# Two PSUM accumulators of a fused attention and mixture kernel: from two banks of one tile to two tiles

## The chip, the core and the metric

The kernel runs on one NeuronCore of a Trainium2 chip. The metric is the device time of one execution in microseconds (us). Runs of this kernel agree closely: three of them lie between 1134.3 and 1134.82 us.

## What is computed

```python
# q, k, v: (4 batches, 8 heads, 576 tokens, 64), float32
scores = (q @ k.T) / 8
mask = scores >= (32nd largest score of the row)
attn = softmax(where(mask, scores, -1e9))
x = attn @ v                                  # 2304 tokens x 512 features
h = maximum(x @ w_in, 0)                      # 512 -> 2048
x = (h * h) @ w_out                           # 2048 -> 512
h = x @ w_in2                                 # 512 -> 2048
out = (h * clip(h + 3, 0, 6) / 6) @ w_out2    # 2048 -> 512, float32
```

## The kernel before, in words

**Number format.** Everything that TensorE (PE) multiplies is held as a high and a low fp16 half, so each product is three matmuls: high times high, high times low, low times high. The four weight matrices arrive as 64-bit numbers. VectorE (DVE) and GpSimd (POOL) turn them into fp32 (lines 372, 375, 431). PE then multiplies each slab with itself so that the matrix's scale can be found (`gram`, line 447). After that, PE and ScalarE (ACT) split the scaled slab into its halves (`w_split`: matmuls at lines 555 and 561, ACT at 558 and 564).

**Attention.** For a tile of 128 queries, PE makes the scores (lines 707 to 716). DVE finds the 32 largest of each row by MAX8 and MATCH_REPLACE8 (lines 754 to 762). ACT and POOL make mask, exponent and halves (lines 766 to 793), a transposing DMA on SP's queue turns them, and PE multiplies with v (line 811).

**The mixture layers.** The 2304 tokens are taken in 18 units of 128 rows; two of the units are put together from two tiles of 64 rows, so the reads of the first layer's accumulator count 20. For one unit and one layer, 4 groups of 4 slices run through these steps. PE makes `hb` (line 1046, 12 matmuls of 128x128 a slice). ACT, and in the second layer DVE, apply the nonlinearity (1053, 1055, 1058, 1061). ACT and POOL split it into `ghl` (1068, 1071). PE adds the slice into an accumulator of 512 fp32 columns (line 1078, three matmuls of 128x512 a slice, called one step below). The first layer's accumulator (m = 0, here accumulator 0) is read by ACT at line 959 (squares for the row scale), by ACT at line 283 (high half) and by DVE at line 287 (low half). A transposing DMA (line 967) then brings the two halves into `hl`, the second layer's operand. The second layer's accumulator (m = 1, accumulator 1) is read by ACT at line 1150, and its result is stored to the output.

**Where the accumulators live.** `acc_t` is one PSUM tile of two banks; `acc_t[:, 0, :]` is accumulator 0 and `acc_t[:, 1, :]` accumulator 1. While the weights are being prepared, the same two banks have other uses: `gram` collects in bank 1, and every third slab of the first two matrices is scaled in bank 0 (`bank = "acc0"` at line 551), read there by ACT.

**What sets the order.** A planner (`Plan.run`) decides once, from costs, priorities and the dependencies that it is given, in which order each engine's instructions are written. Its pools `acc0` and `acc1` are two separate resources. The tile framework underneath then puts the semaphore waits on the written instructions, from what each one reads and writes. Every engine works through its own list in order. On PE, first-layer steps of one unit and second-layer steps of another alternate, with the `hb` matmuls of both between them.

Of the kernel before, what the change touches and what calls it, by code (L numbers as in the profile page):

```python
# [9 lines left out]
F32 = mybir.dt.float32  # L10
F16 = mybir.dt.float16
BF16 = mybir.dt.bfloat16
I32 = mybir.dt.int32
U16 = mybir.dt.uint16
AF = mybir.ActivationFunctionType
# [4 lines left out]
P = 128  # L20
# [115 lines left out]
def tile_topk_attention_moe_moe2(  # L136
# [11 lines left out]
    nc = tc.nc  # L148
# [4 lines left out]
    NT, DM = out.shape  # L153
# [15 lines left out]
    ps = ctx.enter_context(tc.tile_pool(name="ps", bufs=1, space=PSUM))  # L169
# [47 lines left out]
    for name, n in (("av", 1), ("h", 2)):  # L217
        pool(name, n, [P, 512], F32, ps)

    acc_t = ps.tile([P, 2, 512], F32, name="acc")  # L220
    plan.pool(acc0=1, acc1=1)
    pool("S", SBUFS, [P, 2 * S], F32)
    pool("W", 2, [P, S], F32)
# [161 lines left out]
    def w_convert(i, n_, pn, par):  # L385

        loads = wload[i, n_]
        hm = kb(i, 2 * w_order(i)[n_], 2 * w_order(i)[n_] + 2)
        src = kb(PLACE[i][n_][0], 4 * PLACE[i][n_][1], 4 * PLACE[i][n_][1] + 4) if PLACE[i][n_] and is64 else []
        key = n_  # L390
        low = is64 and n_ % 4 < NPOOL[i] and (i < 3 or n_ < 9)
        last = loads
        if is64:
            steps = []

            def conv():
                parts = stage[i, n_]
                w_ = 512 // len(parts)
                if not steps:
                    mid = take("h", "cv")  # L400
                    for h_, words in enumerate(parts):
                        steps.append(bits_to_f32(home(i, n_)[:, w_ * h_:w_ * h_ + w_],
                                                 words.rearrange("p (n a) -> p n a", a=2), low,
                                                 mid[:, w_ * h_:w_ * h_ + w_]))
                for e_ in steps:
                    next(e_)

            c_ = c0_ = None
            for cost in (0.65, 0.66) if low else (0.65, 0.66, 0.66):
                c_ = task("DVE", cost, (f"conv{i}", key), conv, deps=[*loads, c_], reads=src, writes=hm,  # L410
                          alloc=[] if c_ else ["h"])
                c0_ = c0_ or c_
            last = [c_]
            free("h", c0_, c_)
            wconv.append(c_)
            keep_warm(c_, 16 * i + n_)
            if PLACE[i][n_] is None:
                for h_ in range(2):
                    free("stg", loads[h_], c_)
            if low:  # L420

                box = {}

                def low_bits():
                    box["t"] = take("stg").bitcast(I32)[:, 0:512]
                    top = stage[i, n_][0].bitcast(U16).rearrange("p (n a) -> p n a", a=4)[:, :, 1]
                    nc.scalar.activation(box["t"], top, AF.Copy, scale=2.0 ** -13)

                def add():
                    d = home(i, n_).bitcast(I32)  # L430
                    nc.gpsimd.tensor_tensor(d, d, box["t"], op=ALU.add)  # L431

                b_ = task("ACT", 0.52, (f"bits{i}", key), low_bits, deps=[c0_], reads=src, alloc=["stg"])
                a_ = task("POOL", 1.22, (f"add{i}", key), add, deps=[b_], writes=hm)
                free("stg", b_, a_)
                last = [a_]
        ngrp = 4 if i % 2 == 0 else 1
        per = 16 // ngrp
        j = n_ % per

        def gram():
            pn["t"] = acc_t[:, 1, :].rearrange("p (c n) -> p c n", c=4)

            top = home(i, n_).bitcast(BF16).rearrange("p (n a) -> p n a", a=2)[:, :, 1]
            for c in range(4):
                blk_ = top[:, c * P:(c + 1) * P]
                nc.tensor.matmul(pn["t"][:, c, :], blk_, blk_, start=(j, c) == (0, 0), stop=j == per - 1,
                                 skip_group_check=True)

        pn["g"] = task("PE", 0.4, (f"gram{i}", key), gram, deps=last + [pn.get("g", lastgram.get(i - 1))], reads=hm,  # L450
                       alloc=["acc1"] if j == 0 else [])
        lastgram[i] = pn["g"]
        if j == 0:
            pn["o"] = pn["g"]
# [68 lines left out]
    def w_split(i):  # L523


        def diagonal():
            nc.gpsimd.tensor_scalar(diag, ident, wsc[i][:, 0:1], 1.0, op0=ALU.mult, op1=ALU.mult)

        d_ = task("POOL", 0.3, ("norm", 0), diagonal, deps=[wchain[i]], writes=["diag"])
        for n_, s in enumerate(w_order(i)):  # L530
            hm = kb(i, 2 * s, 2 * s + 2)
            key = n_
            box = {}
            if SPE[i][n_ % 4] == "a":
                def scaled(x=home(i, n_), box=box):
                    box["t"] = take("stg")[:, 0:512]
                    nc.scalar.activation(box["t"], x, AF.Copy, scale=wsc[i][:, 0:1])

                def high(hi=wt[i][:, s, 0, :], box=box):
                    nc.scalar.activation(hi, box["t"], AF.Copy)  # L540

                def low(hi=wt[i][:, s, 0, :], lo=wt[i][:, s, 1, :], box=box):
                    nc.gpsimd.tensor_tensor(lo, box["t"], hi, op=ALU.subtract)

                t1 = task("ACT", 0.61, (f"high{i}", key), scaled, deps=[wchain[i]], reads=hm, alloc=["stg"])
                t2 = task("ACT", 0.52, (f"high{i}", key), high, deps=[t1], writes=hm)
                wsplit[i, s] = task("POOL", 1.11, (f"low{i}", key), low, deps=[t2], writes=hm[1:])
                free("stg", t1, wsplit[i, s])
                continue

            bank = "acc0" if i < 2 and n_ % 3 == 2 else "h"

            def scaled(x=home(i, n_), box=box, bank=bank):
                box["t"] = acc_t[:, 0, :] if bank == "acc0" else take("h", "wx")
                nc.tensor.matmul(box["t"], diag, x, start=True, stop=True)

            def high(hi=wt[i][:, s, 0, :], box=box):
                nc.scalar.activation(hi, box["t"], AF.Copy)  # L558

            def rest(hi=wt[i][:, s, 0, :], box=box):  # L560
                nc.tensor.matmul(box["t"], minus, hi, start=False, stop=True, skip_group_check=True)

            def low(lo=wt[i][:, s, 1, :], box=box):
                nc.scalar.activation(lo, box["t"], AF.Copy)  # L564

            t1 = task("PE", 0.95, (f"scaled{i}", key), scaled, deps=[d_], reads=[*hm, "diag"], alloc=[bank])
            t2 = task("ACT", 0.48, (f"high{i}", key), high, deps=[t1], writes=hm)
            t3 = task("PE", 0.22, (f"rest{i}", key), rest, deps=[t2], reads=hm[:1])
            t4 = task("ACT", 0.48, (f"high{i}", key), low, deps=[t3], writes=hm[1:])
            free(bank, t1, t4)  # L570
            wsplit[i, s] = t4
# [360 lines left out]
    def x2_operand(u):  # L932

        us, n = units[u], usize[u]
        several = len(us) > 1
        box = {}
# [15 lines left out]
        def rows(i):  # L952
            return slice(off[i], off[i] + nof[i])

        def square(i):
            if i == us[0]:
                box["ss"], box["yh"] = take("ss"), take("xh")
            r = rows(i)
            nc.scalar.activation(box["yh"][r, 0].bitcast(BF16), acc_t[r, 0, :], AF.Square, accum_out=box["ss"][r],
                                 **({"scale": T["px", i][r]} if several else {}))  # L960

        def total():
# [34 lines left out]
        free("h", t3, t4)  # L997
        lows = []
        for i in us:
            lows += split(DM, lambda r=rows(i): acc_t[r, 0, :], [lambda r=rows(i): box["yh"][r, 0]],  # L1000
                          [lambda r=rows(i): box["yh"][r, 1]], lambda i=i: (T["px", i] if several else box["s"])[rows(i)],
                          "d", (("yhigh", pos[1, u, 0]), ("ylow", pos[1, u, 0])), [t4])
        t6 = task("SP", 1.25, ("yflip", pos[1, u, 0]), flip, deps=lows, lat=WLAT)
# [23 lines left out]
    def group(m, u, g):  # L1027
# [45 lines left out]
        def acc(fi, chunks):  # L1073
            f = g * GF + fi
            gl = [box["g"][:, d, fi * n:(fi + 1) * n] for d in range(2)]
            o_ = acc_t[0:n, m, :]
            for a, d in PRODS:
                nc.tensor.matmul(o_, gl[d], wt[2 * m + 1][:, f, a, :], start=f == 0 and (a, d) == (0, 0),  # L1078
                                 stop=f == KF - 1 and (a, d) == PRODS[-1])
# [56 lines left out]
    def second_layer(u):  # L1136
# [10 lines left out]
        def evac(ch):  # L1147
            rows = min(P, n - ch * P)
            box["o", ch] = take("f", "o")
            nc.scalar.activation(box["o", ch][0:rows], acc_t[0:rows, 1 if n == P else ch, :], AF.Copy,  # L1150
                                 scale=box["oc"][0:rows])

        def store(ch):
# [225 lines left out]
```

## Time and profile before

| what | value |
|---|---|
| median of 3 runs | 1134.74 us (1134.3 to 1134.82) |
| the profiled execution's own time | 1135.86 us |
| its span, first to last instruction | 1134.0 us |
| PE busy | 1032.9 us, 91% |
| DVE, ACT, POOL busy | 83%, 76%, 71% |
| mean granted TensorE clock | 0.98 |

The profiled execution lies 1.12 us above the median of the runs. Busy time of PE is read with care: the ends of matmuls are modelled in the profile, and a record overlaps the start of the next one. An idle time "<-X" is the time in which the engine stood still until X released it.

### The profile page before, as it was taken

How to read it: one execution, taken by the hardware profiler on the slowest of the kernel's cores; microseconds unless marked ns; L12 is line 12 of the kernel's file. 1: busy time of each engine (PE TensorE's matmuls, PEld its weight loads, DVE VectorE, ACT ScalarE, POOL GpSimd, SP SyncE). 2: the span in 40 equal slices, each digit the busy share in tenths (PEclk: the TensorE clock that was granted, in tenths of full speed). 3: DMA queues.
4: the chain of work that ended last, by engine and by line, in shares of the span. 5: the costliest groups of instructions: out<-in, count | busy, mean ns of one | idle time of the engine just before them, and what ended most of it. 6: DMA issues, size and time to landing. Idle time of an engine off the chain costs nothing.

```text
span 1134.0 us, 31149 instructions
## 1 busy us (share of the span) xinstructions
PE 1032.9 (91%) x12407; PEld 723.9 (64%) x12407; DVE 939.9 (83%) x2026; ACT 866.8 (76%) x1600; POOL 802.0 (71%) x1041
## 2 busy tenths in 40 slices
PE   3436988889999999999999999999999999999998
PEld 1234446476766776677666767777767767777675
DVE  6999999999778999999989999986799989970010
ACT  6755989799898777888997878878967878773332
POOL 5798767589877677777887878777767867673221
PEclk9985999989999999999999999999999999999999
DMA  8978655224565424343754334434233332431100
GB/s 273 263 227 282 181 120 139 57 52 66 117 121 124 67 53 68 68 62 64 120 114 96 63 73 66 69 72 86 71 63 62 69 72 53 73 72 41 10 20 20
DMA packets 227905, 107.40 MB, mean 95 GB/s; under 512 B 210736, under 2 KB 210736, under 8 KB 227760
## 3 DMA queue, kind: packets, MB, share of 16 engines
q1 hardware_dynamic: 227760, 105.41, 43.0%
q8 instruction: 97, 1.59, 0.6%
q14 instruction: 48, 0.39, 0.1%
HBM read 48.76 MB, written 4.72 MB: 47 GB/s over the span
## 4 chain that ended last, share of the span: by engine, by line
PE 61%; ACT 15%; DVE 13%; issue 4%; POOL 3%; DMA 3%; SPq 0%; ACTq 0%; DVEq 0%; POOLq 0%
PE acc L1078 25%; PE hb L1046 25%; PE av L811 4%; DVE W L759 3%; PE sp L713 3%; DVE m L762 3%; ACT E L775 2%; ACT w L564 1%; DVE m L754 1%; ACT E L783 1%; ACT w L558 1%; DVE cv L372 1%; DVE w L375 1%; ACT wc L788 1%; POOL w L431 1%
## 5 line engine op out<-in xcount | busy, mean ns | idle before, releaser
L1046 PEld LDWEIGHTS <-w 128*128 128x128 f16 x6912 | 424.3, 98 | 105.3 <-issue 5.9
L1078 PE MATMUL acc<-w,ghl 128*128 128x512 f16 x1728 | 460.0, 379 | 12.0 <-DVE xh L287 5.6
L1046 PE MATMUL hb<-hl,w 128*128 128x128 f16 x6912 | 467.2, 220 | 4.0 <-ACT w L564 1.6
L762 DVE MAX8 m<-W 128x8 f32<-128x576 f32 x432 | 314.2, 749 | 1.8
L778 POOL TENSOR_TENSOR E<-S,E 128x576 f32<-128x576 f32 x144 | 203.3, 1414 | 50.6 <-ACT E L775 49.8
L1071 POOL TENSOR_TENSOR ghl<-r,ghl 128x512 f16<-128x512 f32 x144 | 167.3, 1162 | 100.4 <-ACT ghl L1068 88.4
L759 DVE MATCH_REPLACE8 W<-m,W 128x576 f32<-128x576 f32 x288 | 213.2, 742 | 0.0
L1078 PEld LDWEIGHTS <-ghl 128*128 128x128 f16 x1728 | 145.1, 98 | 100.1 <-issue 14.6
L792 POOL TENSOR_TENSOR wc<-E,wc 128x512 f16<-128x512 f32 x144 | 167.8, 1166 | 39.5 <-ACT wc L788 37.6
L775 ACT ACTIVATE E<-S,scalars 128x576 f32<-128x576 f32 x144 | 111.5, 775 | 35.6 <-POOL scalars L770 33.4
L783 ACT ACTIVATE E<-E,scalars 128x576 f32<-128x576 f32 x144 | 125.1, 869 | 17.0 <-POOL E L778 16.6
L754 DVE MAX8 m<-S 128x8 f32<-128x576 f32 x144 | 107.1, 748 | 22.6 <-ACT S L722 16.4
L1061 DVE SCALAR_TENSOR_TENSOR r<-r,hb 128x512 f32<-128x512 f32 x72 | 48.8, 678 | 78.2 <-ACT r L1055 77.3
L759 DVE MATCH_REPLACE8 W<-m,S 128x576 f32<-128x576 f32 x144 | 106.7, 742 | 0.0
L1068 ACT ACTIVATE ghl<-r 128x512 f16<-128x512 f32 x144 | 90.4, 628 | 19.9 <-DVE r L1061 17.0
L788 ACT ACTIVATE wc<-E 128x576 f16<-128x576 f32 x144 | 98.1, 681 | 0.7
L811 PEld LDWEIGHTS <-wT 128*128 128x128 f16 (+1 forms) x2240 | 82.4, 102 | 19.3 <-issue 6.5
L1055 ACT ACTIVATE r<-hb,bias,scalars 128x512 f32<-128x512 f32 x72 | 55.7, 774 | 47.3 <-PE hb L1046 43.6
L811 PE MATMUL av<-vv,wT 128*128 128x64 f16 (+1 forms) x2240 | 91.0, 196 | 0.7 <-DMA wT<-wc 0.7
L431 POOL TENSOR_TENSOR w<-w,stg 128x512 int32<-128x512 int32 x57 | 72.6, 1285 | 25.1 <-DVE w L375 9.2
L1053 ACT ACTIVATE r<-hb 128x512 f32<-128x512 f32 x72 | 43.1, 598 | 57.2 <-PE hb L1046 56.7
L726 ACT ACTIVATE S<-sp 128x1024 f32<-128x1024 f32 x64 | 65.3, 1020 | 14.5 <-POOL E L778 14.2
(113 smaller groups left out, 1208.2 us busy)
## 6 DMA issues: line engine op xcount, KB each, us to landing
w<-in_moe_w_in_dram SPq DMA_DIRECT2D x32, 512.0 KB, 6.4
w<-in_moe_w_out_dram SPq DMA_DIRECT2D x29, 512.0 KB, 4.2
stg<-in_k_dram SPq DMA_DIRECT2D x16, 320.0 KB, 3.2
stg<-in_v_dram SPq DMA_DIRECT2D x16, 320.0 KB, 3.8
stg<-in_q_dram SPq DMA_DIRECT2D x16, 288.0 KB, 3.9
out_dram<-o SPq DMA_DIRECT2D x16, 256.0 KB, 2.1
wT<-wc SPq DMA_TRANSPOSE x144, 3.3
stg<-in_moe_w_out_dram SPq DMA_DIRECT2D x6, 256.0 KB, 3.5
```

The source lines that it names most:

```text
L754: nc.vector.max(m[:, 0:8], scores())
L759: nc.vector.match_replace(out=T["W", s], in_to_replace=m[:, 8 * c - 8:8 * c], in_values=scores() if c == 1 else T["W", s], imm_value=-3.0e38)
L762: nc.vector.max(m[:, 4 * r:4 * r + 8], T["W", s])
L775: nc.scalar.activation(T["E", s], scores(), AF.Relu, bias=T["kb", s], scale=-FAR)
L778: nc.gpsimd.tensor_tensor(T["E", s], scores(), T["E", s], op=ALU.subtract)
L783: nc.scalar.activation(T["E", s], T["E", s], AF.Exp, bias=T["nb", s], scale=T["scl", b, hp], accum_out=T["sums", i][:, t:t + 1])
L788: nc.scalar.activation(T["wc", s][:, 0:S], T["E", s], AF.Copy)
L792: nc.gpsimd.tensor_tensor(wc[:, S + TAIL:], e[:, 0:S - TAIL], wc[:, 0:S - TAIL], op=ALU.subtract)
L811: nc.tensor.matmul(out_[cols, t * D:(t + 1) * D], wT[0:kr, a, cols], vv[0:kr, vb, hh, c, :], start=n_ == 0, stop=n_ == len(prods) - 1)
L1046: nc.tensor.matmul(box["h"][:, fi * n:(fi + 1) * n], wt[2 * m][:, kk * 4 + f // 4, a, f % 4 * P:(f % 4 + 1) * P], hl[:, c, kk, 0:n], start ...
L1071: nc.gpsimd.tensor_tensor(flat(box["g"][:, 1]), flat(box["r"]), flat(box["g"][:, 0]), op=ALU.subtract)
L1078: nc.tensor.matmul(o_, gl[d], wt[2 * m + 1][:, f, a, :], start=f == 0 and (a, d) == (0, 0), stop=f == KF - 1 and (a, d) == PRODS[-1])
```

## The change

`acc_t` becomes a list of two tiles of one bank each, and every use takes the tile that the index named before. The two tiles lie in the same two banks as before, and the planner is given the same tasks, so each engine's instructions come in the same order as before.

```diff
-    acc_t = ps.tile([P, 2, 512], F32, name="acc")
+    acc_t = [ps.tile([P, 512], F32, name=f"acc{m}") for m in range(2)]
...
-            pn["t"] = acc_t[:, 1, :].rearrange("p (c n) -> p c n", c=4)
+            pn["t"] = acc_t[1].rearrange("p (c n) -> p c n", c=4)
...
-                box["t"] = acc_t[:, 0, :] if bank == "acc0" else take("h", "wx")
+                box["t"] = acc_t[0] if bank == "acc0" else take("h", "wx")
...
-            nc.scalar.activation(box["yh"][r, 0].bitcast(BF16), acc_t[r, 0, :], AF.Square, accum_out=box["ss"][r],
+            nc.scalar.activation(box["yh"][r, 0].bitcast(BF16), acc_t[0][r], AF.Square, accum_out=box["ss"][r],
...
-            lows += split(DM, lambda r=rows(i): acc_t[r, 0, :], [lambda r=rows(i): box["yh"][r, 0]],
+            lows += split(DM, lambda r=rows(i): acc_t[0][r], [lambda r=rows(i): box["yh"][r, 0]],
...
-            o_ = acc_t[0:n, m, :]
+            o_ = acc_t[m][0:n]
...
-            nc.scalar.activation(box["o", ch][0:rows], acc_t[0:rows, 1 if n == P else ch, :], AF.Copy,
+            nc.scalar.activation(box["o", ch][0:rows], acc_t[1 if n == P else ch][0:rows], AF.Copy,
```

What differs in the built program is which instructions wait. In the lists below a name in brackets is the engine whose semaphore the instruction waits for (a name with DMA is a queue's). In the changed kernel `acc_99` is accumulator 0 and `acc_100` accumulator 1; `w_95` is the second layer's output matrix.

PE, in the middle of the mixture, a second-layer step; before:

```order
L1046 MATMUL hb<-hl,w_92 128x128
L1078 LDWEIGHTS ghl
L1078 MATMUL acc<-w_95,ghl 128x512 [waits Activation_49]
L1078 LDWEIGHTS ghl
L1078 MATMUL acc<-w_95,ghl 128x512
L1078 LDWEIGHTS ghl
L1078 MATMUL acc<-w_95,ghl 128x512
```

And in the changed kernel:

```order
L1046 MATMUL hb<-hl,w_92 128x128
L1078 LDWEIGHTS ghl
L1078 MATMUL acc_100<-w_95,ghl 128x512
L1078 LDWEIGHTS ghl
L1078 MATMUL acc_100<-w_95,ghl 128x512
L1078 LDWEIGHTS ghl
L1078 MATMUL acc_100<-w_95,ghl 128x512
```

Nothing moved; the step's first matmul no longer waits for ACT. Over the whole list, 49 of the second layer's matmuls at line 1078 wait for ACT (34) or DVE (15) before, and 7 (ACT) in the changed kernel. Of the first layer's, 13 wait before (8 ACT, 5 DVE) and 14 (DVE) after. PE's `gram` matmuls at line 447 lose all 11 of their waits for ACT.

ACT, at the same place, around its read of accumulator 0 at line 283; before:

```order
L775 ACTIVATE E<-S,scalars 128x576 [waits Pool_49]
L1053 ACTIVATE r<-hb 128x512 [waits PE_49]
L283 ACTIVATE xh<-acc,scalars 128x512 [waits DVE_49,PE_49]
L1058 ACTIVATE r<-r 128x512 [waits Activation_49]
L775 ACTIVATE E<-S,scalars 128x576 [waits Pool_49]
```

And in the changed kernel:

```order
L775 ACTIVATE E<-S,scalars 128x576 [waits Pool_49]
L1053 ACTIVATE r<-hb 128x512 [waits PE_49]
L283 ACTIVATE xh<-acc_99,scalars 128x512 [waits DVE_49]
L1058 ACTIVATE r<-r 128x512 [waits Activation_49]
L775 ACTIVATE E<-S,scalars 128x576 [waits Pool_49]
```

Nothing moved here either; line 283 waits for DVE, which computes its scale, and no longer for PE. Before, 17 of the reads at line 283 and 10 of those at line 287 (on DVE) wait for PE; in the changed kernel none does.

PE, while the weights are prepared, between a slab's `gram` (line 447) and another slab's scaling in bank 0 (line 555); before:

```order
L447 LDWEIGHTS w_93
L447 MATMUL acc<-w_93 128x128 [waits Activation_49]
L447 LDWEIGHTS w_93
L447 MATMUL acc<-w_93 128x128
L447 LDWEIGHTS w_93
L447 MATMUL acc<-w_93 128x128
L447 LDWEIGHTS w_93
L447 MATMUL acc<-w_93 128x128
L555 MATMUL acc<-w_92,diag 128x512
```

And in the changed kernel:

```order
L447 LDWEIGHTS w_93
L447 MATMUL acc_100<-w_93 128x128
L447 LDWEIGHTS w_93
L447 MATMUL acc_100<-w_93 128x128
L447 LDWEIGHTS w_93
L447 MATMUL acc_100<-w_93 128x128
L447 LDWEIGHTS w_93
L447 MATMUL acc_100<-w_93 128x128
L555 MATMUL acc_99<-w_92,diag 128x512 [waits Activation_49]
```

The wait for ACT stands four matmuls later, on the one that writes the bank that ACT reads.

## Rows read from the trace of the kernel before

**Rows 1.** The profile's page: span, busy time of each engine, granted clock in 40 slices.

```profile
span 1134.0 us, 31149 instructions
PE 1032.9 (91%) x12407; PEld 723.9 (64%) x12407; DVE 939.9 (83%) x2026; ACT 866.8 (76%) x1600; POOL 802.0 (71%) x1041
PEclk9985999989999999999999999999999999999999
```

**Rows 2.** Busy time by stretch; PEclk is the granted clock.

```profile
core 0: us, PE busy (x) PEld busy (x) DVE busy (x) ACT busy (x) POOL busy (x), PEclk, DMA share, GB/s
...
80.00:111.00 31.00, 17.76 (x146) 13.23 (x147) 29.61 (x58) 14.92 (x26) 26.83 (x28) 0.50 0.86 271
111.00:170.00 59.00, 51.59 (x376) 27.26 (x375) 54.27 (x116) 53.83 (x103) 39.65 (x46) 1.00 0.59 158
...
226.00:237.00 11.00, 7.07 (x59) 6.15 (x59) 10.93 (x28) 11.00 (x22) 9.93 (x17) 0.54 0.27 51
...
300.00:1010.00 710.00, 699.65 (x8951) 499.84 (x8949) 651.01 (x1420) 578.50 (x1075) 536.77 (x725) 1.00 0.42 78
1010.00:1050.00 40.00, 38.80 (x471) 28.12 (x470) 6.48 (x20) 19.47 (x35) 16.96 (x20) 1.00 0.26 51
1050.00:1134.00 84.00, 77.68 (x848) 55.09 (x847) 10.17 (x23) 26.05 (x41) 17.85 (x17) 1.00 0.09 17
```

**Rows 3.** The chain that ended last, from 300 us on, shares by line.

```profile
by line: PE acc L1078 34.2%; PE hb L1046 32.0%; PE av L811 4.9%; PE sp L713 3.5%; issue 3.0%; DVE W L759 2.6%; DVE m L762 1.9%; PE spare L716 1.3%; PE sp L707 1.0%; ACT r L1055 0.9%; ACT xh L283 0.9%; DVE xh L287 0.9%; DVE m L754 0.9%; ACT 
```

**Rows 4.** Line 1078 (both accumulators): PE's matmuls, idle before them, until whom.

```profile
L1078 PE MATMUL acc<-w,ghl x1728: 376/379/390, 187.6 to 1129.4; 128*128 128x512 f16 x192
...
  DVE xh L287: 5.6, 10
...
  ACT xh L283: 1.9, 6
  ACT xh L959: 1.7, 6
  ACT o L1150: 0.4, 1
```

**Rows 5.** The same line: who waited for PE there (us, times).

```profile
  ACT o L1150: 13.0, 11
...
  DVE xh L287: 6.2, 6
  ACT xh L283: 3.8, 2
```

**Rows 6.** PE's instructions in time, 552.9 to 556.8 us: start, us, what, idle.

```profile
552.93 0.83 PE L1046 MATMUL hb<-hl,w 128*128 128x128 f16 x12
554.41 0.81 PE L1078 MATMUL acc<-w,ghl 128*128 128x512 f16 x3 [0.64 <-ACT xh L283]
555.05 0.83 PE L1046 MATMUL hb<-hl,w 128*128 128x128 f16 x12
556.12 0.81 PE L1078 MATMUL acc<-w,ghl 128*128 128x512 f16 x3 [0.24 <-DVE xh L287]
```

**Rows 7.** ACT and DVE in the same stretch: the reads of accumulator 0.

```profile
553.67 0.69 ACT L283 ACTIVATE xh<-acc,scalars 128x512 f16<-128x512 f32 x1
...
555.32 0.75 DVE L287 SCALAR_TENSOR_TENSOR xh<-acc,scalars,xh 128x512 f16<-128x512 f32 x1 [0.36 <-issue]
```

**Rows 8.** Line 447: PE's idle time (matmuls and weight loads) and until whom.

```profile
  POOL w L431: 59.4, 26
...
  ACT w L564: 1.7, 3
  ACT w L558: 1.4, 2
```

**Rows 9.** PE's waits from 1010 us to the end: us, times, longest.

```profile
PE acc L1078 <- DVE xh L287: 2.4, 3, 0.9
PE acc L1078 <- ACT o L1150: 0.4, 1, 0.4
```

## The prediction

> **What bounds the kernel now.** I read the page first: PE is busy 91% of the span and DVE 83% [rows 1]. The reader is to see that no single share decides, because the stages differ. So I went to the busy time by stretch. From 300 to 1010 us PE is busy 699.65 of 710 us and DVE 651.01; from 1010 us on DVE has 6.48 us in 40 and 10.17 in 84, and PE still 38.80 and 77.68 [rows 2]. The mixture's matmuls on PE are what the time is made of from 300 us on. The chain says the same: over this stretch the PE lines 1078, 1046, 811, 713, 716 and 707 hold 34.2 + 32.0 + 4.9 + 3.5 + 1.3 + 1.0 = 77% of it [rows 3]. Before that, from 111 to 170 us, PE, DVE and ACT are each busy 52 to 54 us of 59, and none leads [rows 2].
>
> Then I asked where PE stands still at line 1078. Of its idle time there, 5.6 us (10 times) end with DVE's read at line 287, 1.9 (6) with ACT's at 283, 1.7 (6) with ACT's at 959 and 0.4 (1) with ACT's at 1150 [rows 4]. One case in time shows what these are. PE's step into accumulator 1 starts at 554.41, when ACT has finished reading accumulator 0 (553.67 + 0.69 = 554.36), after 0.64 us of idle time. The next one starts at 556.12, just after DVE's read of accumulator 0 (555.32 + 0.75 = 556.07), after 0.24 us [rows 6, 7]. The step writes the other bank. It needs nothing of what ACT and DVE read. The tile is shared, and the wait is for the tile.
>
> **The change, part by part.** It adds no instruction, moves none and leaves the banks where they are. It only takes away waits, and what each took is costed here.
>
> *PE's waits in the mixture.* The idle time of the four rows is 5.6 + 1.9 + 1.7 + 0.4 = 9.6 us in 23 stalls [rows 4]. The stall is longer than the idle time that is shown, because a matmul's record reaches over the next one's start: a step's record lasts 0.81 us, but the next matmul starts 555.05 - 554.41 = 0.64 us after it began [rows 6]. So a stall is about 0.81 - 0.64 = 0.17 us longer than shown; with the median record of 379 ns [rows 4] and (0.81 - 0.38) / 2 = 0.215 us between starts it is 0.16. I take 0.16, for the matmuls of line 1046 too, and add 23 x 0.16 = 3.7 us: 13.3 us of stalls. Nearly all are at the second layer's matmuls, whose list of waits falls from 49 to 7; a first-layer step that waited for line 1150's read of accumulator 1 loses its wait as well. How much reaches the end? Nothing, if other engines are late next, and all 13.3, if PE is never short of operands. The share of the chain that PE's lines hold is the row that is nearest: 77% [rows 3], which gives **10.2 us**.
>
> *ACT's and DVE's waits for PE.* DVE's read at line 287 waited for PE 6.2 us (6 times), ACT's at 283 3.8 us (2) [rows 5]. These are waits for steps into accumulator 1 and go away entirely, since accumulator 0 was complete at line 959. They lie right ahead of PE's stalls just counted, in the same hand-over (PE, ACT, PE, DVE, PE), so I cost them at **nothing** more. Their cover is PE's own list, which has the other unit's steps to go on with. If it is gone, at most the two lines' shares of the chain, 0.9% each of 834 us or 7.5 us, could hold such waits [rows 3], and the 10.0 us of idle time cannot give more than that; the low end of the range has room for a part. Line 1150's 13.0 us stay for the greater part: it must wait for the last step of its own accumulator, and only a step of the other one behind that (0.64 us) falls away.
>
> *The weights' stage.* PE's matmuls at line 447 wait 1.7 us (3) and 1.4 us (2) for ACT's lines 564 and 558 [rows 8], which read the other bank. With 5 x 0.16 that is 3.9 us. On the path they are worth nothing at one end and 3.9 us at the other. In this stage PE, DVE and ACT are about equally busy and POOL holds PE for 59.4 us over all of line 447 [rows 2, 8], so I take a quarter, **1.0 us**: four engines share the path.
>
> *Waits that become visible.* The first layer's opening step now waits for DVE's line 287 alone where it waited for ACT or DVE. That is the old accumulator's last reader, which has to end anyhow: nothing. Two of SP's transposes at line 967 name PE as an additional releaser; they wait for old second-layer matmuls that PE passed long before: nothing. If either were late, the `hl` transposes behind it would delay the second layer of that one unit.
>
> *The sum.* 10.2 + 0 + 1.0 = 11.2 us. The profiled execution took 1135.86 us and lies 1.12 us above the median of the runs; against itself the forecast is 1124.7, against the median 1134.74 - 11.2 = **1123.5 us**.
>
> **A rule of the skill.** PE's granted clock is 1.00 from 300 us to the end although PE has all these short stalls [rows 2]. The Trainium skill, "TensorE: Matmul & The Clock Gate", section "A second HAM failure mode: psum-queue depth-cycling", tells of a kernel that steps through PSUM banks and idles briefly between groups so often that its clock swings between its two levels. By that rule the stalls would cost clock as well, and taking them away would give more than the 11.2 us; by the row there is nothing to give back, and the sum stands.
>
> **The rivals.**
> - *Absorbed.* DVE, busy 651 of 710 us up to 1010 us, sets the pace of attention, and PE's earlier steps only wait for operands. Then only the waits after 1010 us pay, where DVE is nearly idle: 2.4 + 0.4 us in 4 stalls [rows 9], with 4 x 0.16 some 3.4 us, so 1131.3 us. For it speaks DVE's load; against it PE's 77% of the chain.
> - *Slower, by the clock.* PE had its lower level, 1.2 of 2.4 GHz, at 80 to 111 us (0.50) and around 226 to 237 us (0.54) [rows 2], the first after and during little work: 17.76 us of 31. With the waits gone PE does its pieces of the weights' stage sooner and then waits longer in one go for POOL's line 431. If its clock then fell at the start of the dense stretch for as long as it did the first time, 31 us, that stretch would lose half of it, 15.5 us: 1134.7 - 11.2 + 15.5 = 1139.0 us. It decides from 22.4 us of additional lower clock in dense work. Against it: the gaps lie in a stage in which the clock stood at 1.00, and their sum does not grow.
> - *Nothing happens.* Each stalled step might find its own operand no earlier than the reader's end, so that another semaphore takes over: 1134.7 us. Against it: in the list of the kernel before, that step has a single wait, for ACT, and its weight loads have none, so its operands were already covered by earlier waits.
> - *All of it.* PE's 13.3 us and the weights' 3.9 us both reach the end: 1117.5 us.
>
> **How the numbers follow.** Forecast 0.70, absorbed 0.15, all of it 0.07, nothing 0.04, slower by the clock 0.04. The range takes in the absorbed case at the top, 1131.5, and reaches towards "all of it" at the bottom, 1118.5; left out are the cases of no gain and half of "all of it", about 0.12, and the tails of the rest. A measurement of this kernel can tell about 0.2%, 2.3 us, from no change. Faster than that are the forecast, "absorbed" and "all of it", 0.92 together; within it lies "nothing" with a small part of "absorbed", 0.05 in all; slower is left with 0.03.
>
> **What would show it.** In the changed profile line 1078 should no longer have idle time ended by lines 287 and 283, and next to none by 959; what ends it next should be POOL's line 1071 or nothing. Lines 283 and 287 should not wait for PE. PE's share of the span should rise by about a point, as its work is the same in a shorter span. The prediction is wrong if these waits are gone and idle time of the same sum stands under other names, above all before lines 713, 811 and 1046 (operands late), or if the granted clock is below 1.00 in a stretch after 240 us.

## The result, and the profile after

The changed kernel takes **1118.58 us** (median of 4 runs, 1116.62 to 1119.72) where the kernel before takes 1134.52 (4 runs, 1132.14 to 1134.82). The ratio is 0.9862 with a 95% interval from 0.9841 to 0.9883, so it is 1.4% faster. Beside the last three experiments below both ran again: 1118.88 against 1134.44, ratio 0.9863 [0.9849, 0.9876]. The forecast was 1123.5 with a range from 1118.5 to 1131.5: the direction was right and the size too small, 11.2 us where 15.9 were measured. The time lies 0.1 us inside the lower end of the range, and two of the four runs lie below it: that the range held it is in part luck.

The profiled execution took 1119.72 us. The head of its page answers to [rows 1]:

```profile
span 1117.9 us, 31115 instructions
PE 1028.1 (92%) x12407; PEld 722.4 (65%) x12407; DVE 941.8 (84%) x2026; ACT 864.8 (77%) x1600; POOL 801.4 (72%) x1041
PEclk9975999989999999999999999999999999999999
```

The span is 16.1 us shorter. Each engine runs as many busy instructions as before, in about the same busy time, and PE's share has risen from 91 to 92%.

Busy time by stretch, for the stretches of [rows 2] from 300 us on:

```profile
core 0: us, PE busy (x) PEld busy (x) DVE busy (x) ACT busy (x) POOL busy (x), PEclk, DMA share, GB/s
...
300.00:1010.00 710.00, 706.88 (x9093) 506.70 (x9092) 654.99 (x1432) 585.38 (x1088) 544.84 (x735) 1.00 0.43 79
1010.00:1050.00 40.00, 40.00 (x481) 29.26 (x479) 4.05 (x12) 16.25 (x28) 12.17 (x13) 1.00 0.20 36
1050.00:1117.90 67.90, 63.78 (x697) 45.23 (x695) 8.47 (x16) 21.05 (x32) 14.11 (x13) 0.99 0.06 17
```

PE is busy 706.88 us of 710 where it was 699.65, and all 40 of the next 40. It gets through 9093 matmuls in the first of these stretches instead of 8951. The granted clock is 1.00, as before; the 0.99 of the last stretch falls after 1114 us, behind PE's last matmul (0.88 from there to the end, 1.00 from 1050 to 1114).

The chain that ended last, from 300 us on, answers to [rows 3]:

```profile
by line: PE acc L1078 37.1%; PE hb L1046 36.6%; PE av L811 5.5%; PE sp L713 3.9%; DVE W L759 2.8%; DVE m L762 2.1%; PE spare L716 1.4%; PE sp L707 1.3%; issue 1.2%; DVE m L754 0.9%; ACT S L726 0.5%; DVE r L1061 0.5%; POOL E L778 0.5%; DMA o
```

PE's lines now hold 37.1 + 36.6 + 5.5 + 3.9 + 1.4 + 1.3 = 86% of it, where they held 77. The reads at lines 283 and 287 are no longer among its larger shares.

Line 1078, PE's matmuls alone, answers to [rows 4, 5]:

```profile
L1078 PE MATMUL acc<-w,ghl x1728: 376/379/390, 187.8 to 1113.4; 128*128 128x512 f16 x192
its engine sat idle before it (us, times) until:
  POOL ghl L1071: 1.3, 3
who waited for it (us, times):
  ACT o L1150: 10.2, 7
  ACT xh L959: 2.9, 3
```

Every idle row that ended with a read of an accumulator is gone. DVE's line 287 and ACT's line 283 wait for this line no more, as forecast. Line 1150 still waits, 10.2 us instead of 13.0, for the last step of its own accumulator. Line 959 waits 2.9 instead of 6.9.

**Where the time came from.** The two kernels have the same instructions in the same order, so the start of each matmul can be set beside its counterpart. Up to 300 us the changed kernel gains 0.3 us. From 300 us on, the matmuls at line 1078 come 16.8 us sooner after the ones ahead of them, in 38 places, and 0.7 us later in three, which makes 16.1 us. Another 0.9 us is given back at one matmul of line 889. With small gains elsewhere it is 15.7 us in all, and 15.8 in the trace of the second time that the changed kernel ran, so the scatter of the times lies mostly before 300 us: in the kernels whose weights' stage is that of the kernel before, the first matmul after it comes at 298.6 to 300.6 us.

These 16.1 us are more than the idle time of [rows 4] and more than the 13.3 us counted in the prediction. The page's group for line 1078 shows why, in the kernel before:

```profile
L1078 PE MATMUL acc<-w,ghl 128*128 128x512 f16 x1728 | 460.0, 379 | 12.0 <-DVE xh L287 5.6
```

and in the changed one:

```profile
L1078 PE MATMUL acc<-w,ghl 128*128 128x512 f16 x1728 | 460.5, 379 | 1.4 <-POOL ghl L1071 1.3
```

The last number group is the idle time. It falls from 12.0 us, in 38 gaps, to 1.4 us, in 4. The rows that name a releaser before add up to 5.6 + 1.9 + 1.7 + 0.4 = 9.6 us for the reads [rows 4] and 1.0 for POOL's line 1071. The other 1.4 us of the 12.0 are 13 gaps of 0.10 to 0.13 us for which the answer names nobody. One of them, from the timeline of the kernel before (start, duration):

```profile
494.86 0.81 PE L1078 MATMUL acc<-w,ghl 128*128 128x512 f16 x3
495.51 0.83 PE L1046 MATMUL hb<-hl,w 128*128 128x128 f16 x12
496.47 0.81 PE L1078 MATMUL acc<-w,ghl 128*128 128x512 f16 x3
...
496.22 0.20 ACT L959 ACTIVATION_READ_ACCUMULATOR xh<-acc 128x1 f32 x1
```

and the same matmuls in the changed kernel:

```profile
492.49 0.81 PE L1078 MATMUL acc<-w,ghl 128*128 128x512 f16 x3
493.14 0.83 PE L1046 MATMUL hb<-hl,w 128*128 128x128 f16 x12
493.81 0.81 PE L1078 MATMUL acc<-w,ghl 128*128 128x512 f16 x3
```

From the first `hb` matmul to the next step it is 496.47 - 495.51 = 0.96 us before and 493.81 - 493.14 = 0.67 us after. The step started 0.05 us after ACT's read of the other bank ended (496.22 + 0.20 = 496.42). It is a stall of 0.29 us, and the row bears no mark of one: all but 0.13 us lie under the modelled end of the `hb` matmul, and the rest has no name. In all, behind 12 of the 13 unnamed gaps the step starts 0.05 us after the end of such a read. With the 23 of [rows 4] that makes 35 stalls, 9.6 + 1.3 = 10.9 us of idle time, and with 35 x 0.16 for the overlap of the records 16.5 us. By the starts of the matmuls these 35 places give 16.6 us.

**What line 889 gives back.** In the changed kernel this matmul waits for DVE:

```profile
937.53 0.18 PE L889 MATMUL pnx<-scalars,ones 128*128 128x1 bf16 x1 [0.76 <-DVE r L1061]
```

DVE had been late since 919.24 us, when a small instruction of its own took 1.13 us. The same two instructions of DVE and POOL in the kernel before:

```profile
929.13 0.17 DVE L865 TENSOR_TENSOR rv<-rv,hsc 128x8 f32<-128x8 f32 x1
929.25 1.17 POOL L1071 TENSOR_TENSOR ghl<-r,ghl 128x512 f16<-128x512 f32 x1 [2.02 <-ACT ghl L1068]
```

and in the changed one:

```profile
919.24 1.13 DVE L865 TENSOR_TENSOR rv<-rv,hsc 128x8 f32<-128x8 f32 x1
919.18 1.16 POOL L1071 TENSOR_TENSOR ghl<-r,ghl 128x512 f16<-128x512 f32 x1 [1.80 <-ACT ghl L1068]
```

Before, DVE starts 0.12 us ahead of POOL and is done in 0.17 us. After, it starts 0.06 us behind POOL and ends 0.02 us after it. PE's stall at line 889 stands in the traces in which this line 865 is long (both of the changed kernel, and the first, third, fifth and sixth experiment) and in none of the other four.

### The profile page after: what moved, and what is told of

It is laid out like the page before. It is cut to its first block, busy times and chain, and to the rows that moved or that the text cites. A ratio compares the mean times of both kernels' runs of the same rounds, so it can differ in the third digit from the quotient of the medians.

```text
span 1117.9 us, 31115 instructions
## 1 busy us (share of the span) xinstructions
PE 1028.1 (92%) x12407; PEld 722.4 (65%) x12407; DVE 941.8 (84%) x2026; ACT 864.8 (77%) x1600; POOL 801.4 (72%) x1041
## 4 chain that ended last, share of the span: by engine, by line
PE 67%; DVE 14%; ACT 11%; issue 3%; POOL 3%; DMA 2%; SPq 0%; POOLq 0%; DVEq 0%; ACTq 0%
PE hb L1046 28%; PE acc L1078 27%; PE av L811 4%; DVE W L759 4%; PE sp L713 3%; DVE m L762 3%; DVE cv L372 2%; DVE w L375 1%; DVE m L754 1%; ACT w L564 1%; POOL w L431 1%; ACT w L558 1%; PE spare L716 1%; ACT E L775 1%; PE sp L707 1%
## 5 line engine op out<-in xcount | busy, mean ns | idle before, releaser
L726 ACT ACTIVATE S<-sp 128x1024 f32<-128x1024 f32 x64 | 65.2, 1019 | 13.9 <-POOL E L778 13.3
```

## The experiments

The seven kernels below keep the one tile of two banks. They only declare, for chosen pairs of instructions, that an instruction working in one bank need not wait for one working in the other. A pair that shares a bank waits as before. The core of the edit is this; each experiment sets the four names of its first line:

```diff
+    PE_FREE_OF, FREE_READERS, WPE, WREAD = ...
+    wrote, read = {0: [], 1: []}, {0: [], 1: []}
+
+    def writes(m, i, w=False):
+        for who, r in read[1 - m][-12:]:
+            if (WPE and who == "w") if w else who in PE_FREE_OF:
+                tc.declare_no_dep(i.ins, r.ins, reason="other bank")
+        wrote[m].append(i)
+
+    def reads(m, who, i):
+        if who in FREE_READERS or who == "w" and WREAD:
+            for w in wrote[1 - m][-64:]:
+                tc.declare_no_dep(i.ins, w.ins, reason="other bank")
+        read[m].append((who, i))
```

`writes(m, ...)` stands around the matmuls into bank `m`, `reads(m, who, ...)` around its reads: "square" is line 959, "high" 283, "low" 287, "out" 1150, and "w" any of the weights' stage. The added lines shift the numbers: line 1078 is 1096 in these kernels, 861 is 879, 865 is 883, 889 is 907, 959 is 977, 283 is 297, 287 is 303, 1061 is 1079, 1150 is 1168. In the fourth and the fifth, whose edit is longer, line 1078 is 1106. The first four ran beside one another, with the kernel before at 1134.86 us (15 runs), and the last three on another chip, with it at 1134.44 (9 runs).

### PE released, the reads kept waiting (n1_pe_free)

```diff
+    PE_FREE_OF, FREE_READERS, WPE, WREAD = ('square', 'high', 'low', 'out'), (), False, False
```

> The kernel before with one tile of two banks; only PE's steps at line 1078 no longer wait for the reads (lines 959, 283, 287, 1150) of the other bank; the reads still wait for PE as before. Theory A (PE sets the pace from 300 us on and works through its list in order, so that every stall at line 1078 is span, also those that the profile does not show as idle): the 38 stalls go, about 16 us off, 1118 to 1120 us, with line 1078's idle time under lines 283, 287, 959 and 1150 gone. Theory B (the hand-over through ACT, DVE and the transposing DMA is what is late, and PE's stalls are only its shadow): the reads are as late as before, so less than 5 us off, 1130 or more. Theory C of the prediction (77% of the visible stalls reach the end): 10 us off, 1124.

Measured: 1122.95 us, ratio 0.9895 [0.9881, 0.9908], so 11.9 us faster. The idle time at the accumulating line is as low as in the changed kernel:

```profile
L1096 PE MATMUL acc<-w,ghl 128*128 128x512 f16 x1728 | 460.9, 379 | 1.4 <-POOL ghl L1089 1.3
```

All the stalls at the line went, as theory A has it, but the time is nearer to theory C's; theory B is out. So PE's own waits are worth 11.9 us of the 15.9, and the rest is not at this line. Set beside the kernel before from 300 us on, its matmuls gain 15.6 us and PE's others lose 3.6: 2.6 at line 889, 0.7 at line 713 and 0.7 at line 1046, with 0.4 gained elsewhere.

### The reads released, PE kept waiting (n2_readers_free)

```diff
+    PE_FREE_OF, FREE_READERS, WPE, WREAD = (), ('square', 'high', 'low', 'out'), False, False
```

> The kernel before; only the reads (lines 959, 283, 287, 1150) no longer wait for PE's steps into the other bank; PE's steps still wait for the reads. Theory A: the reads come earlier by part of a step (0.2 to 0.9 us each), so PE's stalls shrink but do not vanish: 5 to 10 us off, 1125 to 1130, with idle time at line 1078 under 283 and 287 left but smaller. Theory B: nearly the whole gain, 14 us or more off, 1120 or less.

Measured: 1124.54 us, ratio 0.9907 [0.9892, 0.9922], 10.3 us faster, a little over theory A's 5 to 10 and far from theory B's 14. The prediction had costed these waits at nothing. They alone give most of what PE's waits alone give, and 11.9 + 10.3 is more than the whole gain, so the two overlap. A read that need not wait for PE ends sooner, and then PE's wait for that read is short or over. The idle time at the line is 5.2 us instead of 12.0:

```profile
L1096 PE MATMUL acc<-w,ghl 128*128 128x512 f16 x1728 | 460.2, 379 | 5.2 <-ACT xh L977 1.5
```

### Both released in the mixture (n3_mixture_free)

```diff
+    PE_FREE_OF, FREE_READERS, WPE, WREAD = ('square', 'high', 'low', 'out'), ('square', 'high', 'low', 'out'), False, False
```

> The kernel before; both kinds of waits across the two banks gone in the mixture layers, kept in the weights' stage. If the weights' stage gave nothing: 15.5 to 16.5 us off, as the change, 1118 to 1119. If it gave the 1.0 us of the prediction: a microsecond less gain than the change.

Measured: 1119.90 us, ratio 0.9867 [0.9854, 0.9881], 15.0 us faster, about a microsecond less than the change, though the intervals do not part the two. Against the first kernel, the reads' waits are worth 1122.95 - 1119.90 = 3.05 us more when PE's are already gone (3.5 by PE's starts from 300 us on). The traces show how they get to PE. These are rows of the reads' tile, `xh`, with PE released and the reads kept:

```profile
its engine sat idle before it (us, times) until:
  PE acc L1096: 10.2, 14
...
who waited for it (us, times):
  DVE xh L303: 4.5, 4
```

and with both released:

```profile
its engine sat idle before it (us, times) until:
...
  PE acc L1096: 2.9, 3
...
who waited for it (us, times):
  DVE xh L303: 1.6, 3
```

With the reads kept, ACT and DVE wait 10.2 us for PE instead of 2.9, and DVE then waits 4.5 us instead of 1.6 for ACT's half, because it reads the same accumulator after it. DVE is dense up to 1010 us (655.70 of 710 us with the reads kept). Work that it does late comes back to PE as a late operand. One case, with the reads kept, on PE and DVE:

```profile
986.68 0.81 PE L1096 MATMUL acc<-w,ghl 128*128 128x512 f16 x3
988.20 0.16 PE L907 MATMUL pnx<-scalars,ones 128*128 128x1 bf16 x1 [0.71 <-DVE r L1079]
...
987.49 0.66 DVE L1079 SCALAR_TENSOR_TENSOR r<-r,hb 128x512 f32<-128x512 f32 x1
```

and the same instructions with both released:

```profile
985.90 0.81 PE L1096 MATMUL acc<-w,ghl 128*128 128x512 f16 x3
986.55 0.17 PE L907 MATMUL pnx<-scalars,ones 128*128 128x1 bf16 x1
...
985.07 0.67 DVE L1079 SCALAR_TENSOR_TENSOR r<-r,hb 128x512 f32<-128x512 f32 x1
```

DVE's line 1079 starts 0.81 us after PE's step in the one and 0.83 us before it in the other, and only in the one does PE stand still for it. Followed back, with the reads kept:

```profile
950.24 0.60 ACT L977 ACTIVATE xh<-acc 128x512 bf16<-128x512 f32 x1 [0.54 <-PE acc L1096]
955.09 0.69 DVE L1079 SCALAR_TENSOR_TENSOR r<-r,hb 128x512 f32<-128x512 f32 x1 [0.46 <-ACT r L1073]
969.68 1.16 POOL L810 TENSOR_TENSOR wc<-E,wc 128x512 f16<-128x512 f32 x1 [0.68 <-ACT wc L806]
969.86 1.00 DVE L879 TENSOR_SCALAR rv<-sums 128x8 f32<-128x8 f32 x1
971.14 1.35 DVE L883 TENSOR_TENSOR rv<-rv,hsc 128x8 f32<-128x8 f32 x1
```

and with both released:

```profile
968.87 0.16 DVE L879 TENSOR_SCALAR rv<-sums 128x8 f32<-128x8 f32 x1
968.90 1.16 POOL L810 TENSOR_TENSOR wc<-E,wc 128x512 f16<-128x512 f32 x1 [0.89 <-ACT wc L806]
969.30 0.78 DVE L883 TENSOR_TENSOR rv<-rv,hsc 128x8 f32<-128x8 f32 x1
```

ACT's read waits 0.54 us for PE's step into the other bank, and DVE then 0.46 us for ACT's line 1073, which came late behind that read. About half a microsecond late, DVE's line 879 starts behind POOL's line 810 and not ahead of it, and takes 1.00 us instead of 0.16; line 883 behind it takes 1.35 instead of 0.78. These two add 1.4 us to DVE's delay, and some 16 us later PE waits for it.

Six matmuls of PE stand still with the reads kept and not with both released, 2.9 us together. Three of them, 0.54 and 0.87 us at line 889 and 0.58 at line 1046, follow such a long instruction of DVE. At the other three, 0.35 and 0.27 us at line 713 and 0.25 at line 889, the delay of ACT's read (line 959 or 1150) comes through ACT and DVE without one. So some 2.0 of the 2.9 us are a small delay made larger by where DVE's instruction met POOL's.

### The weights' stage alone (n4_weights_free)

```diff
+    PE_FREE_OF, FREE_READERS, WPE, WREAD = (), (), True, True
```

> The kernel before; the waits across the two banks gone in the weights' stage alone (lines 447 to 564), kept in the mixture. Theory: the wait for ACT only moves from line 447 to the matmul of line 555 or 561 four matmuls later, so 0 to 0.5 us, 1134 to 1135. Rival (the prediction's term): 1.0 us off, up to 3.9.

Measured: 1133.31 us (11 runs), ratio 0.9988 [0.998, 0.9997]: 0.3 to 2.3 us faster, about 1.4, where a wait that only moves was expected to give 0 to 0.5. At the `gram` matmuls (line 467 here) ACT no longer ends any idle time:

```profile
L467 PE MATMUL acc<-w x256: 217/218/314, 9.0 to 213.4; 128*128 128x128 bf16 x128
its engine sat idle before it (us, times) until:
  POOL w L451: 26.0, 13
  DVE scalars L487: 0.3, 1
```

Of the 3.7 us that this line gains over the kernel before, however, lines 555 and 561, the scaling of the slabs, take 3.7 back (1.5 and 2.2) in these two traces. The wait for ACT moves four matmuls down PE's list, to where it is needed. The 1.4 us are thus not read off at these lines. That part stays unassigned.

### All waits gone, still one tile (n5_all_free)

```diff
+    PE_FREE_OF, FREE_READERS, WPE, WREAD = ('square', 'high', 'low', 'out'), ('square', 'high', 'low', 'out'), True, True
```

> One tile of two banks as before, but no instruction waits any more for one that works in the other bank, neither in the weights' stage nor in the mixture. If the changed kernel is faster for its waits alone, this kernel takes the same time as the changed one: about 1118.5 us (1117 to 1120), and PE's matmuls at the accumulating line lose 15 to 17 us against the kernel before. If the split also moved something else (where a tile lies, how an address is built), this kernel stays behind the changed one by over 2 us.

Measured: 1118.40 us, ratio 0.9856 [0.9843, 0.987], beside the changed kernel's 1118.88 on the same chip. The accumulating line gains 16.1 us over the kernel before, as in the changed kernel. So the split into two tiles is worth its waits, and beyond them nothing that these runs can tell: 0.5 us is less than the scatter of either.

### PE released from the split's two reads only (n6_pe_free_high_low)

```diff
+    PE_FREE_OF, FREE_READERS, WPE, WREAD = ('high', 'low'), (), False, False
```

> PE does not wait for the split's two reads of accumulator 0 (high half on ACT, low half on DVE) while it writes accumulator 1; every other wait is kept. By the visible idle time of these two lines (5.6 + 1.9 us in 16 stalls, and 0.16 for each) the gain is 10.1 us if all of it reaches the end; by the shifts of PE's starts between the two kernels it is 10.5 us in 19 stalls. Both are less a fifth or so that the still waiting reads cost elsewhere on PE, as they did where all of PE's waits were gone: about 8 us, so 1127 us. At 77% of the visible sum it would be 7.8. The theories are not told apart by this kernel alone but by its sum with the next one: if the stalls are independent the two gains add up to the 11.9 us measured with all of PE's waits gone.

Measured: 1129.01 us, ratio 0.9945 [0.9933, 0.9958], 5.4 us by the medians and 4.8 to 7.6 by the interval. That is less than the 8 expected. Line 1078's matmuls gain 9.0 us from 300 us on, where 10.5 were expected, and other lines of PE lose 1.6. In three places a matmul at the line comes later than before, by 0.2 to 0.7 us: a step that no longer waits for one read arrives sooner at a wait for the next.

```profile
  ACT xh L977: 1.7, 6
  ACT o L1168: 1.5, 3
```

Line 1168, which had 0.4 us in one stall [rows 4], now has 1.5 in three.

### PE released from the square and the output only (n7_pe_free_square_out)

```diff
+    PE_FREE_OF, FREE_READERS, WPE, WREAD = ('square', 'out'), (), False, False
```

> PE does not wait for the square (ACT, accumulator 0) while it writes accumulator 1, nor for the output's read (ACT, accumulator 1) while it writes accumulator 0; every other wait is kept. By the visible idle time of these two lines there are 7 stalls, 1.7 + 0.4 us, with 0.16 for each 3.2 us, at 77% 2.5: about 1132.3 us. By the shifts of PE's starts between the two kernels there are 19 stalls of 6.4 us together, most of them hidden under the modelled end of the matmul before: the matmuls at the accumulating line then come 6 us earlier, and the time is 1129 to 1130 us.

Measured: 1129.94 us, ratio 0.9959 [0.9946, 0.9973], 4.5 us by the medians and 3.1 to 6.1 by the interval, where the named idle time gave 2.5 or 3.2 and the longer count 4.4 to 5.4. The page's idle time at the line is

```profile
L1096 PE MATMUL acc<-w,ghl 128*128 128x512 f16 x1728 | 460.2, 379 | 9.2 <-DVE xh L303 5.7
```

or 12.0 - 9.2 = 2.8 us less, in 18 gaps fewer (20 instead of 38). With 0.16 for each that is 2.8 + 2.9 = 5.7 us, and the matmuls at this line gain 5.65 us by their starts. That is nearly twice the 3.2 us of the seven stalls with a name. The short stalls were real time. The two partial kernels together give 5.4 + 4.5 = 9.9 us by the medians, and the one without any of these waits 11.9; the intervals are too wide to tell these apart. By PE's starts from 300 us on the two give 7.35 + 5.26 = 12.6 us against 12.0: near to a sum, as independent stalls should be. At line 1078 alone they give 9.0 + 5.65 = 14.6 of 15.6 us, because in each of the two some steps only go on to the next wait.

## Why the prediction was right in its direction and too small

**What bounds the kernel: right.** PE's own list sets the time from 300 us on. Of the idle time at line 1078 little came back elsewhere: 0.9 us at line 889, and 0.7 us in three places of line 1078 itself.

**PE's waits in the mixture: the term of 10.2 us was mis-sized.** With PE alone released it measured 11.9. Its mechanism and the 0.16 us per stall held. Its count of 23 stalls did not. The prediction took the rows with a releaser's name for all of them. The page's own 12.0 us of idle time was there to be compared with the 9.6 + 1.0 us of the named rows, and the missing 1.4 us are 13 gaps, 12 of which are stalls of 0.26 to 0.29 us once the overlap of the records is added. So 13.3 us should have been 16.5. The share of 77% is not the reason for the shortfall of this term: with the reads kept, 12.0 of 15.6 us, 77%, got through. That the two shares agree is chance, since what was lost was lost to the reads' waits and not to other lines of the chain. And as a yardstick for the change it was wrong, since with the reads released 15.6 of 16.0 us reached the end. The row of the stretch, PE busy 699.65 of 710 us or 98.5% [rows 2], was the nearer one.

**ACT's and DVE's waits for PE: "nothing" was wrong.** They are worth 3.05 us more on top of PE's. The cover named was PE's own list with the other unit's steps. It was PE itself that paid: late reads made ACT's and DVE's next work late, and PE met it at lines 889, 713 and 1046. Some two thirds of that came where a delay of 0.3 to 0.6 us put a small DVE instruction behind one of POOL's that it had been ahead of. So the term could not have been nothing, but its size could not be read off the idle rows either. Together the two terms are 11.9 + 3.05 = 15.0 us, which the third kernel measured at once.

**The weights' stage: 1.0 us, measured 0.3 to 2.3.** The size fits. The reason given (four engines share the path) was not tested apart, so that it fits may be luck. What the traces show is a wait that moves to the next matmul which needs it.

The measured parts, 15.0 + 1.4 = 16.4 us, stand against 15.9 for the whole change.

**The rivals.** "Absorbed" (1131.3) falls: DVE is as dense as it was, and still PE's stalls before 1010 us were paid out, 11.7 us at line 1078 less the 0.9 us at line 889. "Nothing happens" falls with it. "All of it" (1117.5) came nearest, with a chance of 0.07: it had the right share and the wrong count, and its 3.9 us for the weights' stage made up for the stalls that it missed. "Slower by the clock" did not occur. The granted clock is 1.00 from 300 us to PE's last matmul in both kernels, and the mean clock is 0.980 in both profiled executions. The rule that the prediction weighed from the Trainium skill ("TensorE: Matmul & The Clock Gate", section "A second HAM failure mode: psum-queue depth-cycling") would have had PE's clock swing with some 35 short stalls and rise without them. In these traces it was at its upper level with them and without.

## What to carry to other kernels

A framework that tracks dependencies by tile makes two engines wait for one another over banks that they do not share; look for a short wait on a matmul whose operands are ready, released by a read of something that it does not write. When the stalls of a nearly saturated engine are summed, compare the named rows with the group's whole idle time, count the gaps, and add what the records hide for each one. A wait in both directions is costed as one knot: here either side alone gave some two thirds to three quarters of the gain, and both together gave back what the other engines lost as well. When an engine is late, look at the length of its instructions too, and not only at its waits.

## What had not been expected of the hardware

A matmul that waits for a read starts 0.05 us after the read's end, behind 35 of the 38 gaps at line 1078. A stall of 0.26 to 0.29 us costs its full length, although the timeline shows it without a mark and the page's idle time holds 0.10 to 0.13 us of it.

A stall also seems to make PE's busy time longer, because the record ahead of it is not overlapped. From 300 us on PE is busy 699.65 + 38.80 + 77.68 = 816.1 us before [rows 2] and 706.88 + 40.00 + 63.78 = 810.7 after, 5.5 us less with the same matmuls, near to the 35 x 0.16 = 5.6 us of the stalls that are gone. Over the whole span it is 1032.9 - 1028.1 = 4.8 us.

Line 865 of DVE (128x8) ran 160 times in the ten traces. It took 0.17 us in 113 of them and 0.77 to 1.36 in 47, and each of these 47 started during a TENSOR_TENSOR of POOL and ended 0.02 to 0.03 us after it. MAX8 (line 762) starts during such an instruction most of the time and takes 0.75 us with it and without. What makes the one wait and not the other was not tested.
